# A start-up order for a two-layer convolution and feed-forward kernel: v behind the filter, the last kv tile by halves, copies of y later, one more filter in another buffer

## The chip, the cores and the metric

The kernel runs on one NeuronCore of a Trainium2 chip. The metric is the device time of one execution in microseconds (us), lower is better. TensorE is called PE, VectorE DVE, ScalarE ACT, GpSimd POOL and SyncE SP, as in the profile. PEld is the load of weights into PE.

## The reference, cut to what matters

The model has two layers, each a long convolution with a gate (A) and a feed-forward block with GELU (B), with the same weights in both layers.

```python
def _A_ref(q, k, v, shift_k, ssm_k, ssm_D):      # S = 2048, D = 576, ks = 4
    for t in range(ks):                          # short causal filter over k
        k_shift = k_shift + k_pad[:, t:t + S, :] * shift_k[:, ks - 1 - t][None, None, :]
    kv = k_shift * v
    ...                                          # long causal convolution of kv with ssm_k, by FFT of length 2 S
    y = y + kv * ssm_D[None, None, :]
    return q * y

def _B_ref(x, w_gate, w_up, w_down):             # D = 576, F = 4608
    return (_gelu(x @ w_gate) * (x @ w_up)) @ w_down

x = A_q
x = x + _A_ref(_layernorm(x, axis=-1), A_k, A_v, A_shift_k, A_ssm_k, A_ssm_D)
x = x + _B_ref(_layernorm(x, axis=-1), B_w_gate, B_w_up, B_w_down)
x = x + _A_ref(_layernorm(x, axis=-1), A_k, A_v, A_shift_k, A_ssm_k, A_ssm_D)
x = x + _B_ref(_layernorm(x, axis=-1), B_w_gate, B_w_up, B_w_down)
```

All arrays are bfloat16.

## The kernel before, in words

**Blocks.** The 2048 positions are cut into four blocks of 512 (`BS`), a block into four rows of 128 (`RT`). The convolution is done block by block by a discrete Fourier transform of length 2048 that is written as matmuls: with tiles `T` (sines and cosines, and `nT`, `more` for their negatives) a block of kv or of the filter is taken into four frequency tiles (`KTS` is 0, 2, 1, 3), each with a real and an imaginary part (s). Products of a kv tile (`kc`) and a filter tile (`h0`) are made on DVE (`prod`), and matmuls with the turned tiles `V_`, `nV` take them back (`terms`, lines 1316 to 1320). The first block's filter also has `ssm_D` (`drow`) added to its first row.

**The opening.** Everything up to the first feed-forward matmuls is block 0's convolution and gate. It is not written in execution order: a small planner (`Plan`) holds tasks with an engine, a cost, dependencies, a PSUM bank if one is needed, an earliest time (`ready`) and a priority (`prio`). `plan.order` lays them out greedily by these, and the tasks are then issued in that order. Each engine runs its own instructions in that order; semaphores hold what depends on another engine. The costs, the ready times (`K_AT`, `V_AT`, `HN_AT` for the landings of k, v and the filter) and the priorities therefore decide only the order, not what is waited for.

In order, the opening does this:

- Loads: `sk1` (short filter), `k`, the first filter block `hn` (two DMAs, lines 1101 and 1103), `v`, `drow`, then x of block 0 (`x_b`), block 1's filter (`hn[1]`), and weights. SP issues most of them, ACT issues k and v (lines 227 and 234), POOL issues later loads and the writes of tiles to DRAM (`Hd`, `Kd`).
- Sixteen dummy matmuls, then taps (line 1186): the four rows of the short filter are spread over partitions and copied by ACT into `skc`.
- `kvt` products k times tap on DVE (line 1204), summed by PE matmuls with `ident` or `below` (line 1213); the sum times v on DVE (line 1224) is kv, in v's own tile.
- The filter's transposes on PE (`turned_h`, line 1246), copied by ACT into `hT0`; `drow` is added on DVE (line 1271).
- Filter tiles and kv tiles (`conv.fwd_full`, line 275): 16 times eight matmuls, each copied out of PSUM by ACT (lines 1262 and 1287). A part s of a tile is made whole, both column halves h of 288 (`HW`) together.
- Products per tile (lines 310 to 314), sums and differences of pairs of tiles (line 1307), and the inverse (line 1320). Rows 0 and 2 of y add up the four tiles one after the other; rows 1 and 3 take the differences.
- Per row of y: `factor` on ACT (line 1361) scales y out of PSUM, `gate` on DVE (line 1370) makes x and its sum, `copies` on ACT (line 1380) keep y as bf16 and free the PSUM bank, `square` on ACT (line 1387), `root` on POOL (lines 1395 and 1396), `norm` on DVE (line 1403), PE transposes of xn (lines 1415 and 1417), a copy into `xnT` by DVE or ACT (lines 1422 and 1425). Rows come in the order 0, 2, 1, 3.
- `busy` (line 1341): forty 128 by 128 matmuls of `ident` in ten tasks of low priority, whose result nobody reads.
- Two gate/up tiles begin with the columns of rows 0 and 2 (`half_of`, line 1002, "ps"), and are completed with rows 1 and 3.

**Buffers.** The weight pool `wgu` has three buffers; in the opening two of them hold the filter blocks 0 and 1, so that a weight group waits for the transposes of the filter block in its buffer. The pool `xnT` has two.

**The layers behind.** The feed-forward of a unit (layer, block) runs in three phases of F; gate/up matmuls are on line 1002, down on line 1553. The convolutions of blocks 1 to 3 and of layer 2 are fitted in between (`conv.step`, lines 284, 295, 337).

Of the kernel before, what the change touches and what calls it, by code (L numbers as in the profile page):

```python
# [17 lines left out]
P = 128  # L18
# [114 lines left out]
class Conv:  # L133
# [137 lines left out]

    def fwd_full(self, ps, src, kt, s):
        for i in range(RT):
            for h in range(2):
                self.nc.tensor.matmul(ps[:, h, 0:HW], lhsT=self.fw(kt, s, i),  # L275
                                      rhs=src(i)[:, h * HW:(h + 1) * HW], start=(i == 0), stop=(i == RT - 1))
# [27 lines left out]
    def prod(self, part, K, H, dst=None):  # L304
        nc = self.nc
        pr = self.prp.tile([P, 2, self.D], BF16, tag="prod", name="prod")
        if dst is None:
            dst = pr[:, 0, :]
        if part == 0:
            nc.vector.tensor_tensor(out=pr[:], in0=K[:], in1=H[:], op=ALU.mult)  # L310
        else:
            for s in range(2):
                nc.vector.tensor_tensor(out=pr[:, s, :], in0=K[:, s, :], in1=H[:, 1 - s, :], op=ALU.mult)  # L313
        nc.vector.tensor_tensor(out=dst, in0=pr[:, 0, :], in1=pr[:, 1, :], op=ALU.subtract if part == 0 else ALU.add)  # L314
        return dst
# [372 lines left out]
def ssm_geglu_kernel(ctx, tc, A_q, A_k, A_v, A_shift_k, A_ssm_k, A_ssm_D, B_x, B_w_gate, B_w_up,  # L688
# [394 lines left out]
    with tc.manual_schedule():  # L1083
# [6 lines left out]
        with ExitStack() as es:  # L1090
# [5 lines left out]
            wide = lambda: wpool.tile([P, NKC, fw], BF16, tag="wgu", name="hn")  # L1096

            def load_hn(b):
                hn = wide()
                nd = ND - 1  # L1100
                nc.sync.dma_start(out=hn[:, 0:nd, :],
                                  in_=A_ssm_k[0:nd * P, b * BS:(b + 1) * BS].rearrange("(b p) t -> p b t", p=P))
                nc.sync.dma_start(out=hn[0:D - nd * P, nd, :], in_=A_ssm_k[nd * P:D, b * BS:(b + 1) * BS])
                return hn
# [8 lines left out]
            conv.load_v(0, nc.scalar)  # L1113
            nc.sync.dma_start(out=drow[:], in_=A_ssm_D.unsqueeze(0))
# [64 lines left out]
            vneg = add("ACT", 0.9, vnegs, [vsin], prio=10.0)  # L1179
# [13 lines left out]
            K_AT, V_AT, HN_AT = 5.4, 7.0, 6.2  # L1193
# [75 lines left out]
            for a in opens:  # L1269
                a.deps += [t.deps[0] for t in t0] + [kv0[n] for n in range(2)]  # L1270
            t0[0] = add("DVE", 0.46, lambda: nc.vector.tensor_tensor(out=hT0[0:1, 0, :], in0=hT0[0:1, 0, :], in1=drow[:],
                                                                     op=ALU.add), [t0[0]], prio=20.0)
# [5 lines left out]
            for m in KTS:  # L1278
                K0[m] = []
                for s in range(2):  # L1280
                    def fill_ps(task, m=m, s=s):
                        if s == 0:
                            kc[m] = conv.kcp.tile([P, 2, D], BF16, tag="kc", name="kc")
                        conv.fwd_full(psum(("k", m, s), task), lambda i: conv.vt_[0][:, i, :], m, s)
                    a = later(lambda me: add("PE", 0.99, me(fill_ps), list(kv0.values()) + [tneg if m else tsin], bank=True,
                                           prio=-4.0 * KTS.index(m)))
                    K0[m].append(add("ACT", 0.65, lambda m=m, s=s: nc.scalar.copy(
                        out=conv.halves(kc[m][:, s, :]), in_=held.pop(("k", m, s))[:, :, 0:HW]), [a], lat=0.1, frees=[a]))
# [6 lines left out]
            pA = {}  # L1295
            for m in KTS:
                for part in range(2):
                    def product(m=m, part=part):
                        A[part, m] = conv.ybp.tile([P, D], BF16, tag="yb", name="yb")
                        conv.prod(part, kc[m], h0[m], A[part, m][:])  # L1300
                    pA[part, m] = add("DVE", 1.2, product, K0[m] + H0[m])
            conv.yb = {}

            def pair(part, kt, sg):
                def run():
                    conv.yb[part, kt, sg] = b = conv.ybp.tile([P, D], BF16, tag="yb", name="yb")
                    nc.vector.tensor_tensor(out=b[:], in0=A[part, kt][:], in1=A[part, kt + 2][:], op=ALU.subtract if sg else ALU.add)
                return run
            difference = [add("DVE", 0.38, pair(part, kt, 1), [pA[part, kt], pA[part, kt + 2]])
                          for kt in range(2) for part in range(2)]  # L1310
            for kt in range(2):
                for part in range(2):
                    add("DVE", 0.38, pair(part, kt, 0), [pA[part, kt], pA[part, kt + 2]], prio=-30.0)
# [3 lines left out]
            def terms(ps, i, zs, start, stop):  # L1317
                for n, (lhs, z) in enumerate(zs):
                    for h in range(2):
                        nc.tensor.matmul(ps[:, h, 0:HW], lhsT=lhs, rhs=z[:, h * HW:(h + 1) * HW],  # L1320
                                         start=start and n == 0, stop=stop and n == len(zs) - 1)
            for i in (0, 2):
                steps = []
                for n, m in enumerate(KTS):
                    def part_of(task, i=i, n=n, m=m):
                        ps = psum(("y", i), task) if n == 0 else held["y", i]
                        terms(ps, i, [(conv.lhs(m, s, i), A[s, m]) for s in range(2)], n == 0, n == RT - 1)
                    steps.append(later(lambda me: add("PE", 0.5, me(part_of), [pA[0, m], pA[1, m], vneg] + H0[3] + K0[3],
                                                      bank=(n == 0), prio=4.0 if i else 0.0)))
                chain(steps)  # L1330
                inv[i], opened[i] = steps[-1], steps[0]
            for i in (1, 3):
                def whole(task, i=i):
                    terms(psum(("y", i), task), i, [(conv.lhs(kt, s, i), conv.yb[s, kt, 1]) for kt in range(2) for s in range(2)],
                          True, True)
                inv[i] = opened[i] = later(lambda me: add("PE", 0.99, me(whole), difference + [vneg], bank=True))
# [19 lines left out]
            for j in (0, 2, 1, 3):  # L1356
                hot = 12.0 if j % 2 == 0 else 0.0
# [5 lines left out]
                fa = add("ACT", 0.65, factor, [inv[j], stat[j]] + pluses[-2:-1], lat=0.1, prio=hot)  # L1363

                def gate(j=j):
# [12 lines left out]
                gp = add("DVE", 1.1, gate, [fa], prio=hot)  # L1378
                pluses.append(gp)
                copies[j] = add("ACT", 0.65, lambda j=j: nc.scalar.copy(out=conv.halves(conv.y[0][:, j, :]), in_=held.pop(("y", j))[:, :, 0:HW]),  # L1380
                    [fa], frees=[opened[j]], prio=hot + 8.0 if j == 0 else hot - 10.0)
# [7 lines left out]
                sq = add("ACT", 0.96, square, [gp], lat=0.1, prio=hot)  # L1389
# [7 lines left out]
                rt = add("POOL", 0.85, root, [sq], lat=0.05, prio=hot)  # L1397
# [7 lines left out]
                no = add("DVE", 0.6, norm, [rt], prio=hot)  # L1405
# [12 lines left out]
                tx = later(lambda me: add("PE", 0.55, me(turn_xn), [no], bank=True, prio=hot))  # L1418
                tok = slice(j * P, (j + 1) * P)
                view = lambda j=j: held["xt", j][:].rearrange("p a b -> p (a b)")[:, 0:NKC * P].rearrange("p (b q) -> p b q", q=P)  # L1420
                if j < 2:
                    c = add("DVE", 0.85, lambda tok=tok, view=view: nc.vector.tensor_copy(out=xnT_of[0][:, :, tok], in_=view()),
                            [tx], frees=[tx], prio=hot)
                else:
                    c = add("ACT", 1.15, lambda tok=tok, view=view: nc.scalar.copy(out=xnT_of[0][:, :, tok], in_=view()),
                            [tx], lat=0.1, frees=[tx], prio=hot)
# [4 lines left out]
            t1 = turned_h(1, [loads[1]] + [pA[part, m] for part in range(2) for m in (0, 2)] + H0[3] + K0[3], 0.0, -10.0)  # L1431
            conv.nhr = 6
            conv.hr_free[0] = conv.hr_free[1] = NEVER
            for n in range(3):
                loads.append(add("SP", 2.0, lambda n=n: load_wgu(n), [[], t0, t1][n]))
# [5 lines left out]
            add("ACT", 1.28, lambda: nc.scalar.activation(out=warm[:], in_=conv.pis[:], func=ACT.Gelu_apprx_tanh), [tsin, vsin], prio=20.0)  # L1441
# [7 lines left out]
            order = plan.order({"DVE": 2.2, "ACT": 3.3, "PE": 3.0, "POOL": 3.0, "SP": 4.5})  # L1449
# [202 lines left out]
```

## Time and profile before

| | |
|---|---|
| runs | 937.51, 931.75, 932.42 us; median 932.42 |
| the profiled execution's own time | 932.17 us |
| its span, first to last instruction | 930.4 us |
| PE busy | 917.1 us, 99% of the span |
| gate/up matmuls, line 1002 | 561.1 us |
| down matmuls, line 1553 | 294.1 us |
| the filter hn[0]: issued, landed | 1.14 and 8.01 us |
| k: issued, landed | 0.72 and 4.79 us |
| v: issued, landed | 1.13 and 7.20 us |
| last kv tile's last matmul ends | 32.68 us |
| gate/up tile 0 completed from | 50.00 us on |

Times inside an execution are counted from its first instruction. A busy time of PE overlaps between matmuls, since they are pipelined: the distance from start to start is what a matmul costs in a dense row. In the chain, "issue" is time in which an engine waited for nothing that the profile shows. In a line of instructions the bracket gives the idle time ahead of it and what ended it.

### The profile page before, as it was taken

Reading aid. Unit: us, or ns where it says so; the run is one execution under the profiler, and the core shown is the slowest. Engines: PE = TensorE matmul, PEld = TensorE weight load, DVE = VectorE, ACT = ScalarE, POOL = GpSimd, SP = SyncE. Lnnn points to the kernel's source line nnn. Section 1 sums busy time; section 2 is a strip of 40 time slices with the busy share of each in tenths; the row PEclk is TensorE's granted clock in tenths of the full one; section 3 lists DMA queues with packets and bytes.
Section 4 is the critical chain, followed back from the end, with each engine's and each line's share of the span. In section 5 each row is a group of like instructions: output and inputs, shape, how many; then the busy total and the mean of one; then the engine's idle time right before and its main releaser. Section 6 shows DMA issues by size and latency. Waiting matters only on the chain.

```text
span 930.4 us, 19157 instructions
## 1 busy us (share of the span) xinstructions
PE 917.1 (99%) x8103; PEld 529.7 (57%) x8103; DVE 579.3 (62%) x1102; ACT 325.6 (35%) x594; POOL 140.3 (15%) x306
## 2 busy tenths in 40 slices
PE   8999999999999999999999999999999999999998
PEld 5746465564665655645646546556556556556555
DVE  6876776776898899768988873553333334433332
ACT  6665526543324136252122322451221224321211
POOL 2324101412014003230112101230000002100000
PEclk9999999999999999999999999999999999999999
DMA  9899997327925900991952920690720730797720
GB/s 234 244 239 233 283 258 143 116 54 222 222 66 135 266 2 13 195 303 29 238 180 66 179 77 26 108 208 19 148 83 1 140 91 14 129 215 161 144 67 26
DMA packets 125306, 129.69 MB, mean 139 GB/s; under 512 B 39714, under 2 KB 117411, under 8 KB 125220
## 3 DMA queue, kind: packets, MB, share of 16 engines
q1 hardware_dynamic: 115732, 91.74, 46.8%
q0 software_dynamic: 9200, 35.54, 11.7%
q8 instruction: 63, 1.03, 0.5%
q10 hardware_dynamic: 288, 1.18, 0.4%
q14 instruction: 23, 0.19, 0.1%
HBM read 108.09 MB, written 11.80 MB: 129 GB/s over the span
## 4 chain that ended last, share of the span: by engine, by line
PE 95%; DVE 2%; DMA 1%; ACT 1%; issue 0%; POOL 0%; SPq 0%; ACTq 0%; DVEq 0%
PE gu L1002 60%; PE dn L1553 28%; PE ps L275 2%; PE cps L284 1%; PE cps L337 1%; DMA hn<-in_A_ssm_k_dram 1%; PE ps L1320 1%; PE ps L1213 1%; DVE kc L596 1%; PE cps L295 0%; PE ps L1002 0%; PE ps L1246 0%; DVE ab L302 0%; DVE cd L302 0%; ACT eo L297 0%
## 5 line engine op out<-in xcount | busy, mean ns | idle before, releaser
L1002 PE MATMUL gu<-xnT,wgu 64*128 64x512 bf16 x5148 | 561.1, 376 | 2.2 <-DVE x_c L1595 1.5
L1002 PEld LDWEIGHTS <-wgu 64*128 64x128 bf16 x5220 | 254.9, 94 | 305.5 <-issue 9.8
L1536 ACT ACTIVATE ga<-gu 128x512 f32<-128x512 f32 x256 | 152.8, 597 | 471.6 <-PE gu L1002 465.5
L1537 DVE TENSOR_TENSOR hT<-ga,gu 128x512 bf16<-128x512 f32 x256 | 175.6, 686 | 204.9 <-ACT ga L1536 203.6
L1553 PE MATMUL dn<-wd,hT 128*128 128x288 bf16 x2304 | 294.1, 286 | 0.0
L1553 PEld LDWEIGHTS <-hT 128*128 128x128 bf16 x2304 | 223.5, 98 | 65.3 <-issue 9.3
L834 POOL TENSOR_SCALAR means<-s 128x1 f32<-128x1 f32 x28 | 12.7, 452 | 234.4 <-DVE x_c L1589 205.3
L1597 DVE TENSOR_TENSOR x_c<-x_c,dn 128x576 f32<-128x576 f32 x32 | 24.1, 753 | 30.9 <-PE dn L1553 30.9
L1595 DVE SCALAR_TENSOR_TENSOR x_c<-dn,means,x_c 128x576 f32<-128x576 f32 x28 | 22.7, 815 | 26.8 <-PE dn L1553 26.7
L850 POOL TENSOR_TENSOR rstd<-ve,neghalf_t 128x1 f32<-128x1 f32 x56 | 34.7, 620 | 4.7
L314 DVE TENSOR_TENSOR prod<-prod 128x576 bf16<-128x576 bf16 x72 | 33.0, 458 | 2.5
L1526 ACT ACTIVATE ga<-gu 128x512 bf16<-128x512 f32 x30 | 17.9, 597 | 44.0 <-PE gu L1002 42.1
L297 ACT ACTIVATE eo<-cps 128x576 f32<-128x576 f32 x32 | 20.4, 650 | 25.3 <-DVE ab L302 10.1
L412 POOL DMA_DIRECT2D kr<-Kd x24 | 13.2, 550 | 87.2 <-DVE prod L313 86.1
L1576 DVE TENSOR_TENSOR xn<-x_c,dn 128x576 bf16<-128x576 f32 x15 | 11.3, 752 | 24.0 <-PE dn L1553 23.9
L596 DVE TENSOR_TENSOR kc<-ab,cd 128x288 bf16<-128x288 f32 x64 | 25.7, 451 | 0.0
L416 POOL DMA_DIRECT2D hr<-Hd x36 | 19.4, 540 | 41.2 <-DVE prod L313 39.5
L1528 DVE TENSOR_TENSOR hT<-ga 128x512 bf16<-128x512 bf16 x31 | 13.1, 422 | 18.8 <-ACT ga L1527 18.8
L834 POOL TENSOR_SCALAR nm<-s 128x1 f32<-128x1 f32 x28 | 8.7, 312 | 100.4 <-DVE x_c L886 100.3
L842 ACT ACTIVATE junk<-x_c,nm 128x576 bf16<-128x576 f32 x28 | 21.5, 767 | 4.9 <-POOL nm L834 4.9
L876 ACT ACTIVATE yh<-y,rstd 128x576 f32<-128x576 bf16 x28 | 21.4, 768 | 2.3 <-POOL rstd L850 2.3
L849 POOL TENSOR_SCALAR ve<-ss 128x1 f32<-128x1 f32 x56 | 15.2, 271 | 43.1 <-ACT junk L842 43.0
(164 smaller groups left out, 606.1 us busy)
## 6 DMA issues: line engine op xcount, KB each, us to landing
wgu<-in_B_w_gate_dram SPq DMA_DIRECT2D x45, 576.0 KB, 6.6
wd<-in_B_w_down_dram SPq DMA_DIRECT2D x30, 864.0 KB, 7.5
wgu<-in_B_w_up_dram SPq DMA_DIRECT2D x45, 512.0 KB, 8.2
hr<-Hd POOLq DMA_DIRECT2D x36, 288.0 KB, 7.9
kr<-Kd POOLq DMA_DIRECT2D x24, 288.0 KB, 6.6
Kd<-kc POOLq DMA_DIRECT2D x12, 288.0 KB, 5.0
k<-in_A_k_dram POOLq DMA_DIRECT2D x3, 1008.0 KB, 10.4
wgu<-in_B_w_up_dram SPq DMA_DIRECT2D x45, 64.0 KB, 7.8
```

The lines of the kernel that those rows point to most:

```text
L314: nc.vector.tensor_tensor(out=dst, in0=pr[:, 0, :], in1=pr[:, 1, :], op=ALU.subtract if part == 0 else ALU.add)
L596: nc.vector.tensor_tensor(out=into[k][:, plane, cols], in0=a, in1=b, op=op)
L834: nc.gpsimd.tensor_scalar(out=v["nm"][:], in0=v["s"][:], scalar1=-1.0 / D, scalar2=None, op0=ALU.mult)
L842: nc.scalar.activation(out=junk[:], in_=get_x(), func=ACT.Square, bias=v["nm"][:, 0:1], accum_out=v["ss"][:])
L850: nc.gpsimd.tensor_tensor(out=v["rstd"][:], in0=ve[:], in1=neghalf_t[:, 0:1], op=ALU.pow)
L876: nc.scalar.activation(out=g["yh"][:], in_=conv.y[c][:, j, :], func=ACT.Identity, scale=g["rstd"][:, 0:1], bias=1.0)
L1002: nc.tensor.matmul(cols(pair[:, s, :]), lhsT=w[r0:r0 + HK, k, gi * P:(gi + 1) * P], rhs=cols(xnT[r0:r0 + HK, blk_of[k], :]), start=(k == 0 ...
L1536: nc.scalar.activation(out=ga[:], in_=pair[:, 0, :], func=ACT.Gelu_apprx_tanh)
L1537: nc.vector.tensor_tensor(out=hT[:, fi, :], in0=ga[:], in1=pair[:, 1, :], op=ALU.mult)
L1553: nc.tensor.matmul(acc[:, h, 0:HW], lhsT=hT[:, fi, j * P:(j + 1) * P], rhs=wd[2 * wb + fi // WT][:, fi % WT, h * HW:(h + 1) * HW], start=( ...
L1595: nc.vector.scalar_tensor_tensor(out=xh, in0=acc[:, :, 0:HW], scalar=m_[:, 0:1], in1=xh, op0=op, op1=ALU.add)
L1597: nc.vector.tensor_tensor(out=xh, in0=xh, in1=acc[:, :, 0:HW], op=ALU.add)
```

## The change

1. v's load is issued by SP, behind the two loads of the filter, instead of by ACT; `drow` by ACT, behind k, instead of by SP. `K_AT`, `V_AT`, `HN_AT` are 4.9, 8.2, 6.3.
2. The last kv tile (3) is made by column halves: `fwd_part` makes both parts s of 288 columns, ACT copies them, and the products, the second pair's differences and the inverse are tasks by halves. Its DVE operations for one half are 128x2x288 or 128x288.
3. The extra priority of rows 0 and 2 (`hot`) is gone, and copies of y have priority -10.
4. Block 1's filter goes into a buffer of `xnT`; `load_wgu(1)` then has no dependency, `load_wgu(2)` depends on block 0's transposes.
5. Priorities of the V negatives, of `drow`'s addition and of block 1's transposes, and DVE's first free time in the plan (1.9), differ. ACT's load of the GELU table depends on `T` alone.

```diff
+    def fwd_part(self, ps, src, kt, h):
+        for s in range(2):
+            for i in range(RT):
+                self.nc.tensor.matmul(ps[:, s, 0:HW], lhsT=self.fw(kt, s, i),
+                                      rhs=src(i)[:, h * HW:(h + 1) * HW], start=(i == 0), stop=(i == RT - 1))
...
-    def prod(self, part, K, H, dst=None):
+    def prod(self, part, K, H, dst=None, cols=slice(None)):
...
-            nc.vector.tensor_tensor(out=pr[:], in0=K[:], in1=H[:], op=ALU.mult)
+            nc.vector.tensor_tensor(out=pr[:, :, cols], in0=K[:, :, cols], in1=H[:, :, cols], op=ALU.mult)
...
-            wide = lambda: wpool.tile([P, NKC, fw], BF16, tag="wgu", name="hn")
-                hn = wide()
+                hn = (xtp if b else wpool).tile([P, NKC, fw], BF16, tag="xnT" if b else "wgu", name="hn")
...
-            conv.load_v(0, nc.scalar)
-            nc.sync.dma_start(out=drow[:], in_=A_ssm_D.unsqueeze(0))
+            conv.load_v(0, nc.sync)
+            nc.scalar.dma_start(out=drow[:], in_=A_ssm_D.unsqueeze(0))
...
-            vneg = add("ACT", 0.9, vnegs, [vsin], prio=10.0)
+            vneg = add("ACT", 0.9, vnegs, [vsin], prio=-20.0)
-            K_AT, V_AT, HN_AT = 5.4, 7.0, 6.2
+            K_AT, V_AT, HN_AT = 4.9, 8.2, 6.3
...
-                                                                     op=ALU.add), [t0[0]], prio=20.0)
+                                                                     op=ALU.add), [t0[0]], prio=30.0)
...
-                        conv.fwd_full(psum(("k", m, s), task), lambda i: conv.vt_[0][:, i, :], m, s)
+                        (conv.fwd_part if m == KTS[-1] else conv.fwd_full)(
+                            psum(("k", m, s), task), lambda i: conv.vt_[0][:, i, :], m, s)
...
-                        out=conv.halves(kc[m][:, s, :]), in_=held.pop(("k", m, s))[:, :, 0:HW]), [a], lat=0.1, frees=[a]))
+                        out=kc[m][:, :, s * HW:(s + 1) * HW] if m == KTS[-1] else conv.halves(kc[m][:, s, :]),
+                        in_=held.pop(("k", m, s))[:, :, 0:HW]), [a], lat=0.1, frees=[a]))
...
+                for part, h in [(part, None) for part in range(2)] if m != KTS[-1] else [(part, h) for h in range(2) for part in range(2)]:
...
+                    pA[part, m, h or 0] = step = add("DVE", 1.2 if h is None else 0.75, product, (K0[m] if h is None else [K0[m][h]]) + H0[m])
...
+                    difference[h].append(add("DVE", 0.24, pair(part, 1, 1, h), [pA[part, kt, h] for kt in (1, 3)]))
...
+                    for hs in [range(2)] if m != KTS[-1] else [range(1), range(1, 2)]:
...
-                inv[i] = opened[i] = later(lambda me: add("PE", 0.99, me(whole), difference + [vneg], bank=True))
+                    steps.append(later(lambda me: add("PE", 0.5, me(whole), difference[h] + [vneg], bank=(h == 0))))
...
-                hot = 12.0 if j % 2 == 0 else 0.0
...
-                    [fa], frees=[opened[j]], prio=hot + 8.0 if j == 0 else hot - 10.0)
+                    [fa], frees=[opened[j]], prio=-10.0)
...
-            t1 = turned_h(1, [loads[1]] + [pA[part, m] for part in range(2) for m in (0, 2)] + H0[3] + K0[3], 0.0, -10.0)
+            t1 = turned_h(1, [loads[1]] + [pA[part, m, 0] for part in range(2) for m in (0, 2)] + H0[3] + K0[3], 0.0, -30.0)
...
-                loads.append(add("SP", 2.0, lambda n=n: load_wgu(n), [[], t0, t1][n]))
+                loads.append(add("SP", 2.0, lambda n=n: load_wgu(n), [[], [], t0][n]))
...
-            add("ACT", 1.28, lambda: nc.scalar.activation(out=warm[:], in_=conv.pis[:], func=ACT.Gelu_apprx_tanh), [tsin, vsin], prio=20.0)
+            add("ACT", 1.28, lambda: nc.scalar.activation(out=warm[:], in_=conv.pis[:], func=ACT.Gelu_apprx_tanh), [tsin], prio=20.0)
...
-            order = plan.order({"DVE": 2.2, "ACT": 3.3, "PE": 3.0, "POOL": 3.0, "SP": 4.5})
+            order = plan.order({"DVE": 1.9, "ACT": 3.3, "PE": 3.0, "POOL": 3.0, "SP": 4.5})
```

## The prediction, as it was made before the changed kernel ran

> **What bounds the kernel now.** I read the page's shares and chain first, then five stages of the span, then what TensorE (PE) waited for in the opening, then that stretch line by line, and last the DMA queues.
>
> ```profile
> PE 917.1 (99%) x8103; PEld 529.7 (57%) x8103; DVE 579.3 (62%) x1102; ACT 325.6 (35%) x594; POOL 140.3 (15%) x306
> PE 95%; DVE 2%; DMA 1%; ACT 1%; issue 0%; POOL 0%; SPq 0%; ACTq 0%; DVEq 0%
> ```
>
> PE bounds the whole. Nothing in the change takes matmul columns away, so it can win only where PE idles, does fill-in work, or runs slowly. The stages (length; busy of PE, PEld, DVE, ACT, POOL; granted clock; DMA share; GB/s) say where that is:
>
> ```profile
> 0.00:8.05 8.05, 4.08 (x24) 2.54 (x24) 5.78 (x13) 4.79 (x7) 1.97 (x11) 1.00 0.79 265
> 8.05:15.77 7.72, 7.71 (x53) 5.33 (x54) 2.87 (x6) 3.95 (x6) 0.00 (x0) 1.00 1.10 247
> 15.77:32.68 16.91, 16.91 (x138) 13.29 (x136) 14.89 (x35) 11.97 (x21) 8.45 (x16) 1.00 1.13 270
> 32.68:50.00 17.32, 15.57 (x185) 12.41 (x185) 12.94 (x33) 10.89 (x19) 5.21 (x11) 1.00 0.71 186
> 50.00:930.00 880.00, 872.87 (x7707) 496.17 (x7707) 542.82 (x1017) 294.01 (x542) 124.63 (x268) 1.00 0.58 134
> ```
>
> 880 of the 930 us are the layers behind the opening. In the changed program PE's last 7448 of 8103 matmuls stand in the same order, so I take those 880 us as they are. The opening has idle time in three places, PE's own waits:
>
> ```profile
> PE ps L1246 <- DMA hn<-in_A_ssm_k_dram: 2.9, 1, 2.9
> PE ps L1002 <- DVE xnT L1422: 0.9, 1, 0.9
> PE ps L1320 <- ACT kc L1287: 0.7, 1, 0.7
> ```
>
> The last wait ahead of the front is the filter's landing (hn). The line view adds that the work behind it is slow:
>
> ```profile
> 8.05 2.94 PE L1246 MATMUL ps<-ident,hn 128*128 128x128 bf16 x20 [2.85 <-DMA hn<-in_A_ssm_k_dram]
> 10.93 2.58 PE L1213 MATMUL ps<-kvt,below 128*128 128x288 bf16 x10
> 13.31 1.19 PE L1213 MATMUL ps<-kvt,ident 128*128 128x288 bf16 x6
> 14.78 1.14 PE L275 MATMUL ps<-h,T 128*128 128x288 bf16 x8
> 15.77 0.41 PE L1213 MATMUL ps<-kvt,below 128*128 128x288 bf16 x2
> ```
>
> Ten 288-column matmuls take from 10.93 to 13.31, 240 ns each; from 14.78 on eight take 0.99, 123 ns each. The single starts put the turn at 13.9, although the granted clock reads 1.00 throughout. So a microsecond won before that turn is a slow one.
>
> **The front: v behind the filter.** v's one load moves from ACT's queue (L234, 0.46 to issue) to SP's, behind hn's two; the bias row drow goes the other way (0.43). Before, ACT's ring (q10: k, then v) ran against SP's (q1: hn). Packets, MB and share, first for 4 to 6 us, then for 6 to 7:
>
> ```profile
> q10 hardware_dynamic: 126, 0.54, 67.7%
> q1 hardware_dynamic: 249, 0.25, 36.8%
> ...
> q1 hardware_dynamic: 290, 0.29, 87.6%
> q10 hardware_dynamic: 32, 0.07, 18.7%
> ```
>
> hn is 576 packets of 1 KB. 27 passed before 4.0, 249 in 4 to 6 beside v, 290 in 6 to 7 as v ended; it landed at 8.01, a microsecond after its last packet. k was almost through by 4.0. With v behind it, the 549 packets left go at the rate of an undisturbed microsecond (9 to 10: 368 packets): 1.5 us, last packet 5.5, landing 6.6. Bounds: 8.0 (nothing won), and 6.6 itself from below, since PE is in other matmuls until then (next but one paragraph). v's 0.59 MB follow at 0.37 MB/us: through by 7.1, landing 8.1 instead of 7.20. Its cover is the first multiply by v (L1224), at 11.4 in the new order; only a landing after that would stall.
>
> Behind v on SP stand x_b, block 1's filter and the gate/up weights. Their bytes keep their place behind v's, so x_b lands near its old 9.61, and its statistics run at 14. SP's wait for v (1.2 us, ahead of the second weight load) becomes one for drow.
>
> The new order also sets four kv matmuls ahead of the filter's transposes. Their product ends at 5.6 (first product starts at 4.88 and takes 0.75), so they fill 5.62 to 6.6. Then: 20 transposes 2.88, 12 slow kv matmuls at 240 ns 2.88, eight transposes of T 0.45, the first filter tile 0.98. Before: 8.05 + 2.88 + 3.40 + 0.45 + 0.98 = 15.77. After: 6.64 + 2.88 + 2.88 + 0.45 + 0.98 = 13.83. Won: 1.94. This needs the turn at 12.4, which is 5.8 us after the first transpose as in the row of before. If it stays at 13.9, the last 1.5 us run at half pace and 0.7 is lost: won 1.2. DVE follows: the sixth kv product now precedes drow's addition instead of following it, and none of them is late for PE. ACT's table load (1.28) moves to 10.6, into its wait for the transposes of T; if it ran late, V's copy would, and the first tile with it.
>
> 15.77 to 32.68 is dense PE work with ACT following 0.04 behind each tile. I carry its 16.9 us over unchanged.
>
> **The tail: halves, copies.** The last kv tile comes by column halves. The same 16 matmuls, two ACT copies of the same 576 elements (0.64). Products can start after the first copy, 0.98 earlier. DVE's price: per half one 2x288 operation (0.45, the 576 row), then four of 128x288 in bf16, which no row shows. Bounds are 0.15 (half of 0.30, what 1152 costs over 576: 0.75 against 0.45) and 0.45; I take 0.30, the straight line through both rows. Two halves cost 2.95 against 2.39, so the products end 0.98 - 0.56 = 0.4 earlier and the first factor (L1361) starts at +3.4 instead of +3.9, counted from the last kv-tile matmul.
>
> With the copies yielding, ACT does: factors of rows 1 and 3 at +6.35, 2 x 0.65; three squares, 3 x 0.86; then a copy, 0.63: done at +10.85. PE's transposes of xn need the bank that this copy frees, so they begin at +10.9, where before they began at 42.75 - 32.68 = +10.07. That is the new wait; behind it on PE stand all transposes of xn and the gate/up halves, and ACT's and DVE's xnT copies wait for those. In exchange all four rows go at once (4 x 0.81 = 3.24). The first gate/up half starts at +14.13 instead of +12.74 (2.07 long), block 1's remaining ten transposes take 0.83, and the second half starts at +17.03. Before, two rows of transposes (1.7) and the 0.85 wait for xnT stood there: +17.32. Won: 0.3.
>
> **Block 1's filter in xnT's buffer** takes SP's waits for transposes away. The second weight group is asked for at 6.8 instead of 11.0, the third near 29 instead of 42.2, in a stretch where DMA was nearly idle. Nothing: PE first needs the third group near 67. POOL's load of x(1) goes behind the last two roots and is issued at about the old 44.3.
>
> **Sum.** 1.94 + 0.29 = 2.2 us. The profiled execution took 932.17 (span 930.4, 1.8 around it), 0.25 under the median of the runs, 932.42. 932.17 - 2.2 = 930.0; on the median's scale **930.2**.
>
> **Rivals.**
> *The pace turns earlier.* PE is now busy from 3.0 to 5.05 and from 5.62 on, with no long idle. If the turn comes at 10.5, 1.9 us more run at 123 instead of 240 ns: 0.95 further, 929.2. Against it: before, 4 us of work from 1.07 on left the pace slow.
> *hn lands no earlier*, because its own packets are slow to start (issued at 1.14, first seen after 3.6). Then only the four kv matmuls are won, with the turn at 13.9: 0.5 there and 0.3 in the tail, 931.6. For it: hn's late first packets. Against it: 290 packets a microsecond once v ended. [...]
> *The pace falls back* (the slower side). The 40 fill-in matmuls (L1341), spread over 40.3 to 45.4 before, stand in one burst now, ended by +10.2. Up to +14.13 only transposes and waits follow, 4 us; the longest such stretch of before was 47.5 to 50.0, 2.5 us, and the pace held. If it falls, the first gate/up matmuls run at half pace until it turns again, between 2.9 us (first kv matmul to turn) and 5.8 us (first transpose to turn) later: 1.5 to 2.9 lost. From 4.5 us on it eats the 2.2; at 5.8 the time is 933.1. [...]
>
> **How the numbers follow.** Forecast 0.45 (its own range 929.6 to 930.9, by the turn), earlier pace 0.15, hn no earlier 0.20, fallen pace 0.15, something in the layers behind 0.05. The range 928.7 to 933.2 holds all but the last and the outer ends. A measurement of this kernel tells about 1%, 9.3 us, from no change; the whole opening has less to give, so within 1% is 0.96, slower 0.03, faster 0.01.
>
> **What would show it.** hn's landing before 7 and transposes at 6.6; four kv matmuls ahead of them; the turn from 240 to 123 ns near 12.4; products of the last tile in eight operations of 0.30; xn's transposes waiting for ACT's y copy; gate/up half matmuls still at their 57 ns spacing after that. Wrong: hn at 8, half-pace gate/up matmuls near 46, or a changed length behind 48.

## The result, and the profile after

The changed kernel took 939.41 us (median of 7 runs, 937.94 to 944.06) against 932.59 for the kernel before on the same chip (7 runs, 931.75 to 937.51): a ratio of 1.0076, 95% interval 1.0048 to 1.0104. It is slower; 930.2 had been forecast, and 933.2 was the top of the range. Its profiled execution took 937.94 (span 936.2), that of before 932.17 (span 930.4): 5.8 us to find.

The page first, the lines for busy time and for the chain:

```profile
PE 920.4 (98%) x8103; PEld 531.9 (57%) x8103; DVE 580.1 (62%) x1109; ACT 325.7 (35%) x594; POOL 140.3 (15%) x306
PE 95%; DVE 2%; ACT 1%; issue 1%; POOL 1%; DMA 0%; ACTq 0%; DVEq 0%; SPq 0%
```

They say little: still 8103 matmuls, still PE in 95% of the chain. The stages say where. The columns are those of before (length; busy of PE, PEld, DVE, ACT, POOL; granted clock; DMA share; GB/s), cut at the same events: 8.05, the end of the first filter tile, the last kv-tile matmul, the second gate/up half.

```profile
0.00:8.05 8.05, 6.57 (x40) 4.17 (x41) 6.01 (x14) 4.81 (x8) 1.97 (x11) 1.00 0.75 249
8.05:13.03 4.98, 4.98 (x38) 3.56 (x38) 2.63 (x6) 4.49 (x5) 0.00 (x0) 1.00 1.10 280
13.03:29.85 16.82, 16.82 (x138) 13.30 (x136) 15.17 (x36) 11.41 (x22) 8.35 (x16) 1.00 1.26 164
29.85:56.20 26.35, 19.25 (x185) 14.48 (x184) 12.77 (x39) 10.98 (x19) 5.33 (x11) 0.81 1.06 198
56.20:935.00 878.80, 872.83 (x7710) 496.37 (x7708) 543.56 (x1018) 293.98 (x542) 124.70 (x268) 1.00 0.58 135
```

The front is 2.74 us shorter (13.03 against 15.77) and the dense stage as long as it was (16.82 against 16.91). The tail takes 26.35 instead of 17.32, 9.0 more, with a granted clock of 0.81. What lies behind has kept its 880 (936.2 less 56.20). One more number stands in the third line: 164 GB/s, where that stage had moved 270, at a higher DMA share.

The tail on PE, as the timeline has it (start, length, instructions, idle time before and its releaser):

```profile
37.67 2.39 PE L1366 MATMUL ps<-ident 128*128 128x128 bf16 x40 [0.18 <-ACT yh L1385]
46.13 0.61 PE L1441 MATMUL ps<-ident,xn 128*128 128x128 bf16 x4 [6.07 <-DVE xn L1427]
51.39 4.02 PE L1008 MATMUL ps<-xnT,wgu 64*128 64x256 bf16 x36
56.20 1.19 PE L1008 MATMUL ps<-xnT,wgu 64*128 64x256 bf16 x18
```

PE is idle for 6.07 us between the fill-ins and the transposes of xn, and slow behind it: the 40 transposes last from 46.13 to 51.39 (5.26; four rows at the old pace are 3.24), the 36 gate/up matmuls 4.02 instead of 2.14. The list of waits, read upwards from PE, says who was late:

```profile
POOL v L234 <- issue: 13.8, 1, 13.8
...
DVE xn L1427 <- POOL rstd L1420: 7.3, 3, 6.4
...
PE ps L1441 <- DVE xn L1427: 6.1, 1, 6.1
```

PE waits for xn, xn for the square roots on POOL, and POOL stands for 13.8 us ahead of one DMA, the load of v for the second layer (L234). "issue" names no instruction as releaser. The trace's semaphore records give one: in this program POOL's transfers signal their landing on eight semaphores in turn (111 to 118); v(1) is the ninth transfer and waits on the first's, 111, from 28.86 to 42.71. Here the first is the load of k for that layer, k(1):

```profile
16.23 0.76 POOL L229 DMA_DIRECT2D k<-in_A_k_dram  x1
...
43.24 0.54 POOL L234 DMA_DIRECT2D v<-in_A_v_dram  x1 [13.83 <-issue]
```

k(1) was asked for at 16.23 and landed at 42.68, after 26.5 us; v(1) followed 0.56 later. Before, k(1) was asked for at 18.96 and landed at 29.37, after 10.4. The squares that the roots wait for were done by 39.99; the roots ran from 44.57 on, behind v(1) and the write Kd behind it. Why was k(1) slow? The DMA queues for 26 to 40 us, packets, MB and share; first after, then before. q0 is POOL's queue, q1 is SP's, which in this stretch carries the DMA transpose of the third filter block, natural(2), in packets of 256 bytes:

```profile
q0 software_dynamic: 384, 1.81, 67.1%
q1 hardware_dynamic: 779, 0.20, 41.3%
```
```profile
q0 software_dynamic: 925, 3.97, 74.7%
q1 hardware_dynamic: 842, 0.66, 14.2%
```

In both kernels the transpose's packets begin near 22. Before, they were alone (1246 packets in 22 to 24, 766 in 24 to 26) and through at 26.3; POOL's first packet came at 26.2, when 2275 of the transpose's 2304 had started, and then POOL moved 3.97 MB in 14 us. After, POOL's first packet came at 23.1, with 349 of them through. From there both crawl: 38 packets of q1 in 24 to 26, and 1.81 MB of q0 in 26 to 40. natural(2) landed at 51.0 instead of 29.3.

### The profile page after: what moved, and what is told of

The parts are those of the page before. It is cut to its first block, busy times and chain, and to the rows that moved or that the text cites. A ratio compares the mean times of both kernels' runs of the same rounds, so it can differ in the third digit from the quotient of the medians.

```text
span 936.2 us, 19163 instructions
## 1 busy us (share of the span) xinstructions
PE 920.4 (98%) x8103; PEld 531.9 (57%) x8103; DVE 580.1 (62%) x1109; ACT 325.7 (35%) x594; POOL 140.3 (15%) x306
## 4 chain that ended last, share of the span: by engine, by line
PE 95%; DVE 2%; ACT 1%; issue 1%; POOL 1%; DMA 0%; ACTq 0%; DVEq 0%; SPq 0%
PE gu L1008 60%; PE dn L1577 28%; PE ps L281 1%; PE cps L290 1%; PE cps L343 1%; PE ps L1008 1%; PE ps L1218 1%; DVE kc L602 1%; PE cps L301 0%; PE ps L1340 0%; PE ps L1251 0%; DVE ab L308 0%; DVE cd L308 0%; ACT eo L303 0%; DMA xnT<-xn 0%
```

## The experiments

Theories, as the expectations name them. **T1**: the faster front starts k(1)'s load 2.7 us earlier; its packets meet natural(2)'s transpose, both collapse, POOL stands at v(1), the roots are late, PE idles, and its pace falls. **T2**: the new order of the tail costs by itself. **T3**: the earlier weight loads disturb the transpose. **T4**: the collision holds PE by other data than the roots. **T5**: k(1) is late because it is issued ahead of the writes. Where the texts let v(1) wait for k(1), that is so because k(1) is the first transfer on POOL. The ratios are to the kernel before on the same chip (932.31, 932.08, 932.57 and 931.97 on the four chips).

### Is it the collision?

**k(1) later.** In the changed kernel k(1) waits for the first kv tile:
```diff
+            lk1.deps += K0[0]
```


> The changed kernel with one dependency more: the load of k for the second layer, k(1), is emitted on POOL behind the four square roots of the first kv tile instead of ahead of them, so it is issued near 21 us instead of 16.2; everything else stays. T1 (k(1)'s packets meet the DMA transpose of natural(2), both collapse, and POOL stands at the load of v(1), which waits for k(1)): k(1) lands near 30 again, v(1) no longer holds POOL, the last two roots run by 37 to 42, PE's 6.07 us wait for xn shrinks to about 1, gate/up half matmuls go at 57 ns at once; time 928.6 to 930 (the 2.7 won in front and 0.3 in the tail stay). T2 (the order of the tail, copies yielding and one burst of fill-in matmuls, is what costs): the wait for xn and the slow stretch stay, 937 to 938. T3 (the earlier weight loads disturb the transpose, whatever k(1) does): natural(2) still lands near 51 and k(1) late, 936 to 938.

Measured 928.94 (928.03 to 932.81, 10 runs), ratio 0.9969 (0.9960 to 0.9978). One line takes the loss away and leaves a gain: T2 and T3 fall. Not all is clean. In the profiled run, the slowest, POOL's first packet still came at 23.8, since the write Hd(0) now goes first (17.56); natural(2) landed at 37.26, and PE waited 2.2 for xn. v(1) was issued at 34.98, behind the landing of Hd(0) at 34.42 and ahead of that of k(1) at 38.69: what it waits for in these runs is POOL's first transfer, whichever that is.

**k(1) earlier, in the kernel before.** The load is emitted behind the last kv product and stands first on POOL:
```diff
+                        if i0 and j == 0:
+                            conv.load_k(1, nc.gpsimd)
...
-            lk1 = add("POOL", 0.6, lambda: conv.load_k(1, nc.gpsimd), mults, prio=-20.0)
+            lk1 = None
```


> The kernel before with one step moved: k(1)'s load is emitted right behind the last of layer 1's first kv products and stands first on POOL, so it is issued near 17 instead of 18.97; nothing of the change is in it. T1: its first packet now falls inside natural(2)'s DMA transpose (22 to 26.3), which then takes till 45 to 51 instead of 29.3, k(1) lands after 40 instead of 29.4, v(1) holds POOL, the last roots come late, PE idles 4 to 6 us ahead of xn's transposes: 935 to 938. T2 (tail order) and T3 (weight loads): as the kernel before, 932.2 to 932.6, since neither the tail nor the weights are touched.

Measured 937.01 (931.80 to 940.87, 10 runs), ratio 1.0050 (1.0035 to 1.0064). Nothing of the change is in this kernel, only a load issued at 16.94 instead of 18.97, and it loses 4.7 us of the 6.8 that the change loses. In the profiled run k(1) landed at 39.6, natural(2) at 45.1. That run, 934.70, is among the fastest, and the expected wait of 4 to 6 us for xn is not in it: PE waited 1.2 for ht (block 1's filter) and 0.4 for xn, and the granted clock fell for one step.

**natural(2) first.** In the changed kernel the transpose goes ahead of all gate/up weights:
```diff
+            loads.append(add("SP", 6.0, lambda: natural(2)))
             for n in range(3):
...
-                if n == 1:
-                    loads.append(add("SP", 6.0, lambda: natural(2)))
-            wg0 = loads[2]
+            wg0 = loads[3]
```


> The changed kernel with one step moved on SP: natural(2) (the DMA transpose of the third filter block and its write-back) goes ahead of all gate/up weights instead of behind the second group, so its packets go near 13 to 18 instead of from 22 on, and no packet of POOL's queue (first at 23.0 in the changed kernel) falls among them. POOL's order is untouched, k(1) is still issued near 16.2. T1, made sharper by the run with k(1) moved (there the first written tile Hd 0, issued at 17.6, still fell among the transposes, and the profiled run still lost some 4 us): all loss goes, POOL does not stand at v(1), xn's wait is about 1 us; the opening's gain of 2.8 in front and what the tail gives remain: 927.8 to 929.0 in every run, with a narrow spread. T2 (tail order) and T5 (k(1) is simply late because it is issued ahead of the writes): 936 to 939. The weights land some 4 us later than now (26 and 31), still ahead of the gate/up halves near 46, so nothing is expected of that.

Measured 928.95 (928.62 to 929.98, 6 runs), ratio 0.9961 (0.9947 to 0.9974): all of the loss gone, a narrow spread. k(1), still issued early, at 16.65, landed at 27.06, and T5 falls with it. In 26 to 40 us POOL's queue and SP's, which now carries weights there, moved 4.81 MB together: here two busy queues without a transpose did not collapse. POOL's line for v(1) in this run:

```profile
31.27 0.54 POOL L234 DMA_DIRECT2D v<-in_A_v_dram  x1 [0.74 <-PE ps L275]
```

**natural(2) last**, behind the opening and two down weights: the step is taken out of the loop above and put ahead of `natural(3)`.

> The changed kernel with natural(2) moved the other way, behind the opening, just ahead of natural(3) and behind the first two loads of down weights on SP. T1: k(1), Hd and Kd meet no transposes and land as in the kernel before (near 28 to 30) or sooner; v(1) does not hold POOL; the xn wait shrinks to about 1 and PE's pace holds: the opening is 2.8 to 4 shorter, 928 to 929.5, unless natural(2) is late there for layer 2 or meets x(1)'s load of POOL's queue (issued near 44) instead, which would give back 1 to 5 us behind 60. T2: 937 to 938.

Measured 929.46 (928.29 to 930.01, 6 runs), ratio 0.9962 (0.9949 to 0.9976). Ahead of POOL's packets or behind them, it comes to the same.

**natural(2) first, in the kernel before**, the same edit without the change:

> The kernel before with natural(2) ahead of the gate/up weights on SP, and nothing else: what the moved step is worth without the change, so that the change's own worth without the collision is read as the difference to the changed kernel with the same step moved (928.95). T1: in the kernel before the collision costs nothing in most runs (k(1)'s first packet 26.0, transposes through at 26.3; POOL reaches the roots at 39.7 with slack), so 931.5 to 932.4; the change without collision is then worth 2.5 to 3.4. If moving natural(2) gains something by itself, as it would if the transposes or the weights had been on the path before: 929 to 930.5, and the change would be worth little even without collision.

Measured 932.01 (931.26 to 933.00, 11 runs), ratio 0.9998 (0.9989 to 1.0007). The moved step is worth nothing clear of noise by itself. So the change without the collision is worth 2.6 to 3.1 us: 928.95 is 3.13 under its kernel before, and the moved step alone was 0.56 under its own.

**The roots ahead of v(1).** In the changed kernel v(1) and the last Kd wait for the roots; k(1) still collides:
```diff
+                lv1.deps.append(rt)
+                kd3.deps.append(rt)
```


> The changed kernel with POOL's order of the tail changed: the load of v(1) and the write of the last kv tile (Kd 3) are emitted behind the last two roots; k(1) is still issued near 16.2. T1 predicts both halves of its chain apart: the collision stays (k(1) landing near 42, natural(2) near 51), but nothing stands ahead of the roots, so they run by 37 to 41, xn is ready near 41, PE's wait for xn is about 1 instead of 6.07 and the slow gate/up stretch is gone; v(1) is issued near 43, and layer 2's work has it in time: 929.5 to 931.5. T4 (the collision itself holds PE by some other data, x, weights or Kd): PE still idles, 935 to 938. T2 (tail order): 937 to 938.

Measured 935.14 (928.19 to 941.55, 10 runs), ratio 1.0031 (1.0007 to 1.0055): not the 929.5 to 931.5 of T1 as I had put it. In the profiled run (931.55) the chain was cut as expected: roots from 36.4 on, and no wait of PE for xn in its list. But other runs took as long as the changed kernel, so the collision can hold PE by other data too, as T4 has it. DVE's timeline shows one such route:

```profile
42.93 0.76 DVE L1253 COPY ht<-ps 128x1152 bf16<-128x1152 bf16 x1 [1.64 <-DMA Hd<-h]
```

DVE turns block 1's filter into a buffer (ht) that the first written tile, Hd(0), must leave; that write, behind k(1) in POOL's queue, landed at 42.84. DVE stood for 1.64 us, and PE for 1.5. That a later landing makes up the longest runs was not seen, since only one was profiled.

### Which part of the change does it?

**The front alone** (v on SP, drow on ACT, the order that follows):


> The kernel before with the front alone changed (v behind the filter on SP, drow on ACT, the order that follows); halves, copies and the filter's buffer stay as before. T1: the front wins 2 to 2.7 until the first filter tile, k(1) is issued near 16.2 and meets the transposes; POOL reaches v(1) late, and whether that costs depends on how late against the roots, which here are wanted near 37 (39.7 less the front's gain): v(1) held beyond 37 gives 931 to 936 and a wide spread. T2 (the tail's order): no part of the tail is changed, the front's gain stays, 929.5 to 930.3, narrow.

Measured 940.90 (938.74 to 942.93, 4 runs), ratio 1.0091 (1.0076 to 1.0106): by itself at least as slow as the whole change, whose interval overlaps, and the direction is T1's though the size was not foreseen. The route is the one just seen, at full size; the old order of the tail has this copy ahead of xn. The longest waits of PE and of DVE:

```profile
PE ps L1246 <- DVE ht L1248: 10.6, 1, 10.6
```
```profile
DVE ht L1248 <- DMA Hd<-h: 11.7, 1, 11.7
```

Hd(0) landed at 48.78, and v(1) was issued at 48.59. **The front alone, with natural(2) first:**

> The kernel before with the front alone changed (v behind the filter, drow on ACT, the order that follows) and natural(2) ahead of the weights; halves, copies and the filter's buffer as before. If the prediction's front was right apart from the collision: 932.2 less 1.9, 930.3; by the traces of the changed kernel (first filter tile done 13.03, 14.15, 13.46, 12.13 in four of them against 15.77, 14.95 of before's front, some 2.2 on the mean): 929.8 to 930.3. If the front only wins together with the tail's order: 931.5 or more.

Measured 929.70 (929.36 to 931.05, 10 runs), ratio 0.9977 (0.9968 to 0.9987), 2.3 under its kernel before.

**The filter's buffer alone:**


> The kernel before with the filter buffer part of the change alone: block 1's filter in xnT's buffer, the third weight group no longer behind the transposes of T1. The prediction gave this part nothing. T1: SP runs through its list without a wait, and on POOL k(1) comes to stand ahead of the roots, issued near 16 to 17 instead of 18.97, so its first packets fall among the transposes: POOL stands at v(1), 934 to 938, with a wide spread from run to run. T2 (tail order): no part of it is in, 932.3.

Measured 932.40 (931.62 to 938.09, 10 runs), ratio 1.0006 (0.9991 to 1.0020), not the 934 to 938 of T1. The collision is there (k(1) issued at 16.22, landed at 35.38; natural(2) at 45.95), but in nine of ten runs it costs nothing, and POOL's lines in the profiled one say why:

```profile
35.95 0.55 POOL L234 DMA_DIRECT2D v<-in_A_v_dram  x1 [3.25 <-issue]
...
40.16 0.22 POOL L1394 TENSOR_SCALAR ve<-ss 128x1 f32<-128x1 f32 x1 [3.01 <-ACT junk L1386]
```

With the old front and tail the first root has its square only near 40, and v(1) was through by 36. By this trace a collision costs what it runs over that point. In the changed kernel the first square is ready near 36.4 (the first root of the run with the roots ahead of v(1)), and v(1) held POOL until 43.

**The copies alone:**


> The kernel before with one part of the change alone: ACT's copies of y yield to the factors and squares. k(1) is still issued near 18.9. T2 (this order is what costs): slower, 935 or more, with PE idle ahead of xn's transposes and slow gate/up matmuls behind. T1: no collision, and the time is what the order of the tail gives, worked out from rows as 0 to 1 less than before: 931.5 to 932.4.

Measured 931.62 (930.90 to 932.35, 10 runs), ratio 0.9991 (0.9982 to 1.0000): 0.5 better by the medians, and nothing of T2. (Even here k(1), at 18.14, met the transpose in the profiled run: v(1) at 38.9.)

**The halves alone, with natural(2) first:**


> The kernel before with the last kv tile by halves alone, and natural(2) ahead of the weights; copies, front and filter buffer as before. By the prediction the halves bring the first factor 0.5 earlier, less what the later waits give back: 931.7 to 932.2. If they carry more of the gain: 931.3 or less. If eight smaller products cost more than they win: 932.5 or more.

Measured 932.78 (931.75 to 933.69, 10 runs), ratio 1.0007 (0.9998 to 1.0017): no gain. By the medians the parts come to -2.3 (front), -0.5 (copies), 0.3 (buffer) and 0.8 (halves), less than the whole. Only the front's is clear of its interval, and the copies and the buffer were run with natural(2) in its old place. The halves may need the new order of the copies to be worth their eight products; that combination by itself was not run, and why the parts do not add up stays open.

### Why did 6 us of waiting cost 9?

**Fill-ins over the wait**, in the changed kernel: the last of ten fill-in steps has 112 matmuls instead of 4.

> The changed kernel with 108 more fill-in matmuls (their results are read by nothing) in the last of the ten fill-in steps, which covers the stretch from 40 to 46 in which PE waits for xn; loads and POOL's order are untouched. It tells the idle time apart from the slow pace behind it. If the slow pace (40 transposes in 5.26 instead of 3.24 us, 36 gate/up matmuls in 4.02 instead of 2.14) comes from PE having been idle for 6 us, both go back to their old durations and 3.5 to 4 us of the loss are won back: 934 to 934.5 on the scale of the changed kernel's profiled 937.9. If the pace falls for another reason (DMA traffic, the transposes themselves), the time stays at 937.9, or goes up by what the fillers run over.

Measured 941.84 (938.17 to 945.17, 4 runs), ratio 1.0100 (1.0080 to 1.0121): inconclusive. In its profiled run the collision was worse (v(1) at 51.05), and PE stood for 7.9 us in the midst of the fill-ins, from 42.97 to 50.89, with "issue" as releaser; what held it there is not shown. A wait of changing length can't be filled; so I made one of fixed length without the collision.

**Nine roots**, in the changed kernel with natural(2) first:
```diff
+                    for _ in range(9 if j == 0 else 1):
                         nc.gpsimd.tensor_scalar(out=ve[:], in0=v["ss"][:], ...)
                         nc.gpsimd.tensor_tensor(out=v["rstd"][:], ...)
```


> The changed kernel with natural(2) first (no packets of POOL's queue among the transposes, 928.95 measured), and the idle time put back by hand: the first of the four roots is computed nine times over on POOL, so xn's transposes start near 46.5 instead of 41.7, without any slow transfer. It asks what the 6 us of idle PE cost beyond themselves. If the slow stretch of the changed kernel (40 transposes in 5.26 instead of 3.24, 36 gate/up matmuls in 4.02 instead of 2.14) comes from the idle time alone: delay 4.8 plus 3.9 of slow matmuls, less some 0.5 that other waits give back: 936.5 to 937.7, and a granted clock below 1 in 45 to 55. If it comes from the DMA traffic or the transposes: delay alone, 933.5.

Measured 939.47 (939.02 to 940.01, 4 runs), ratio 1.0078 (1.0062 to 1.0093). That is 1.8 above the upper end of what was expected, because a root takes 0.96 here: eight more delayed the second row of xn's transposes to 48.59, a wait of 6.53. The pace fell with no slow transfer about: gate/up matmuls 3.81, granted clock 0.50 from 46.05 to 56.29.

**Nine roots, 76 more fill-ins:**


> The run with nine roots, and 76 more fill-in matmuls (their results are read by nothing, 60 ns each by the 40 of the row) that cover PE's wait until about 46. If idle time is what lowers the pace: transposes of xn again in 3.24, gate/up half in 2.14, granted clock 1.00 throughout, 3.9 less than with nine roots alone: 933 to 934. If the pace falls for another reason, or if these fill-ins do not count: the same as with nine roots alone, within 0.5.

Measured 938.94 (938.49 to 939.28, 4 runs), ratio 1.0070 (1.0056 to 1.0084), not the 933 to 934 expected, since the fill-ins ended at 44.8 and the wait at 48.5. The clock fell all the same, one step later, at 49.69; the gate/up half took 3.95.

**Nine roots, 128 more fill-ins:**


> As the run with nine roots and fill-ins, with 52 fill-ins more, so that they end near 47.8 instead of 44.8 and less than one us of idle is left ahead of xn's last transposes (near 48.5). In all traces so far the granted clock changes only at whole steps of 3.41 us after its first rise, and it fell to 0.50 at the end of a step in which PE had run no matmul but transposes (changed kernel: 41.66 to 45.07, none; nine roots: 42.63 to 46.05, none; nine roots and fill-ins: 46.27 to 49.69, ten transposes). If that is the rule: granted clock 1.00 throughout, the transposes behind the wait in their full-speed time and the gate/up half in 2.14 instead of 3.95: about 2.5 to 3.5 less than the 938.9 of the shorter fill-ins, 935.5 to 936.5. If the pace falls for the DMA traffic or for another reason: 938.9 again, with the clock at 0.50 near 50.

Measured 936.02 (935.62 to 936.52, 4 runs), ratio 1.0043 (1.0026 to 1.0059), 2.9 under the run with too few. The gate/up half is back at 2.14, and the clock holds; the windows' line for 44 to 50 us (PE busy, then the other engines, granted clock 1.00):

```profile
44.00:50.00 6.00, 5.20 (x81) 4.43 (x79) 2.43 (x5) 1.76 (x2) 5.05 (x12) 1.00 1.21 252
```

The same long waits of ACT and DVE, the same transfers, the same transposes: what differs is PE's idleness, busy for 5.20 of these 6 us where it was 2.51 in the run with too few. So in these runs it is idleness that lowers the pace (gate/up half 3.95 there, 2.14 here). The two medians are from different chips; each against its own kernel before, nine roots make it 6.9 slower without fill-ins and 4.05 with these, so about 3 us are the clock.

## Why the prediction was wrong, step by step

**The front: right, and a little small.** hn landed at 6.09 (forecast 6.6), v at 8.46 (8.1), and PE's lines are the forecast order:

```profile
5.56 1.12 PE L1218 MATMUL ps<-kvt,below 128*128 128x288 bf16 x4 [0.36 <-ACT skc L1193]
6.48 2.96 PE L1251 MATMUL ps<-ident,hn 128*128 128x128 bf16 x20
9.37 1.62 PE L1218 MATMUL ps<-kvt,below 128*128 128x288 bf16 x6
10.79 0.98 PE L1218 MATMUL ps<-kvt,ident 128*128 128x288 bf16 x6
...
13.03 0.41 PE L1218 MATMUL ps<-kvt,below 128*128 128x288 bf16 x2
```

Four kv matmuls at 5.56, transposes at 6.48 without a wait for hn, the first filter tile done at 13.03 (forecast 13.83). The front alone measured 2.3, where 1.94 had been worked out. The rival that hn would land no earlier did not come.

**The turn of the pace: the wrong clock was read.** I timed it from the first transpose (5.8 us). The trace's records of the granted clock show it changing, from its first rise on, only at whole steps of 3.413 us: it rose at 10.94 in the profiled run, and the records that follow are 34.13, 10.24 and 880.64 us long, that is 10, 3 and 258 steps. Where the steps fall differs from run to run: the first rise came between 8.93 and 13.94 in eleven traces with the new front, between 11.86 and 15.50 in six with the old. With it the first filter tile ended at 12.13, 13.03, 13.46, 14.15 and 14.75 in five traces, around my 13.83. The earlier pace was a rival of 0.15; it is no case of its own, but the spread of every front.

**"I carry its 16.9 us over unchanged": right for PE, and the failed step.** PE's stage kept its length, 16.82. What I carried over with it was POOL's queue: k(1) would be asked for 2.7 us earlier, and I gave that no price, having looked for what earlier transfers could collide with on SP only. I had the rows: transposes from 22.0 to 26.3, POOL's first packet at 26.2, 7.3 us after its issue. The old front kept them apart by chance, by the last 29 packets of the transpose. And I had asked what stands behind a waiting instruction for PE and ACT, not for POOL, where v(1) waits for the first transfer to land and the roots stand behind it. What came in place of a price of nothing: k(1) 26.5 us under way instead of 10.4, POOL held for 13.8, PE idle for 6.07, and a granted clock of 0.50 behind. Neither the range nor a rival held this.

One reading of rows was wrong too, without cost. I put the third weight group near 29, in a stretch where DMA was nearly idle. Before, the windows have 424 GB/s in 28 to 30 us and some 300 to 400 up to 38; only 38 to 44 is nearly idle. In the changed kernel that group was asked for at 51.62, behind natural(2).

**The tail: right once the collision is away.** With natural(2) first, xn's transposes begin at 41.68, 10.71 after the end of the last kv-tile matmul at 30.97 (forecast 10.9), the first gate/up half 13.72 after it (14.13), the second 16.65 (17.03). The wait for ACT's y copy that I had named is there, 0.49. The 128x288 products took what I had put down for them, 0.30; the trace's group, columns as on the page:

```profile
L319 DVE TENSOR_TENSOR prod<-kc,h 128x288 bf16<-128x288 bf16 x4 | 1.0, 301 | 0.0
```

The factor came at 3.43 (3.4). Won in the tail 0.67 against 0.3. With front and tail the sum for the change alone was 2.2, measured 2.6 to 3.1.

**Block 1's filter in xnT's buffer, "Nothing":** right in time (932.40), wrong in one word: it does change POOL's order, k(1) going first at 16.22, and is harmless for the slack at the roots alone.

**The pace falls back:** the rival's effect came, not by its cause. It needed 4 us of transposes and short waits; what came was 6.07 us of idleness. Loss by rows, profiled run against the one with natural(2) first: the wait ends 16.28 instead of 10.71 after the last kv-tile matmul (5.57), the transposes take 5.26 instead of 3.01 (2.25), from there to the second half 4.81 instead of 2.93 (1.88). Together 9.70; in that other run the last kv-tile matmul came later by 1.12, and 8.6 is the difference of the two profiled times (937.94 and 929.32). The changed kernel's wait and the steps around it, one step of the clock to a line (the granted clock, third column from the end, goes from 1.00 to 0.50):

```profile
38.24:41.66 3.42, 1.82 (x33) 1.65 (x30) 0.81 (x4) 2.81 (x8) 0.00 (x0) 1.00 1.10 223
41.66:45.07 3.41, 0.00 (x0) 0.00 (x0) 0.00 (x0) 0.00 (x0) 1.49 (x4) 1.00 1.12 187
45.07:48.48 3.41, 2.35 (x20) 1.72 (x21) 2.07 (x4) 0.92 (x1) 3.16 (x7) 0.50 1.59 100
```

A step whose 1.82 us of busy PE are all fill-ins, and the next is still at full speed; a step without a matmul, and the next is at half. In the run with the roots ahead of v(1), the steps look like this:

```profile
41.70:45.12 3.42, 1.89 (x26) 1.36 (x26) 1.91 (x3) 1.39 (x2) 1.74 (x4) 1.00 1.30 148
45.12:48.53 3.41, 3.41 (x34) 2.36 (x34) 0.76 (x1) 1.21 (x2) 0.00 (x0) 0.50 1.40 66
```

Here PE was busy for 1.89 of the step, all of it transposes of xn (the first gate/up matmul starts at 45.39), and the clock fell as well. So the rival was near. In the run with natural(2) first, the step of the transposes held its clock (40.57 to 43.99), with fill-ins until 41.18 and PE busy for 2.93 in all. Fill-ins were not enough by themselves: in the kernel before with k(1) early, a step with 0.65 us of them and 1.27 of transposes, PE busy for 1.85, lost its clock, so the rule in the last expectation above, a step of nothing but transposes, is too narrow. What decides whether a step keeps its clock is not shown: 1.82 us of fill-ins kept it, these 1.85 us of both and the 1.89 of transposes did not.

## What to carry to other kernels

When a stage gets faster, list every transfer that it triggers, on every queue, with its first and last packet, and look at what runs in that stretch; that two queues just miss each other, here but for 29 packets, may be chance. For each in-order queue, write down what stands behind a transfer that waits until an earlier one has landed, be it only for its semaphore: here the roots behind v(1), each under 1 us, held the whole tail, and a buffer that waits for a write was second in line. And before a version is dropped as slower, move the transfer that it collides with: the same change with one step of SP's order moved beats both kernels, 928.95 against 932.08.

## What the runs showed of the hardware that I had not expected

- Packets of POOL's queue that came among the DMA transpose natural(2) slowed both queues here, far beyond sharing: in 26 to 40 us the two moved 2.0 MB in the changed kernel, against 4.6 in the kernel before, where the transpose had ended. It varies from run to run: v(1) was issued at 35.0, 35.9, 38.9, 40.2, 43.2, 48.6 and 51.1 in seven profiled runs with the collision, each of another kernel. natural(3), asked for from 41.0 on beside POOL's load of x(1), took 16.2 us to land in the run with natural(2) first, and no wait of PE followed in its list to 70 us.
- POOL's first packet came 7.3 us after its issue before (18.96 to 26.22), 6.9 after (16.23 to 23.10) and 4.9 with natural(2) first (16.65 to 21.51).
- In these traces the granted clock moved in steps of 3.413 us whose phase changed from run to run (first rise at 10.94 in the changed kernel, at 13.90 in the kernel before). Ahead of that rise the profile's row reads 1.00, though in the kernel before the pace was half (240 ns a matmul of 288 columns, 123 behind it): there is no record there.
